# A spectral mixer with a gated feed-forward: the last plain chunk's down stage moves from behind the third new period to behind the second

## The chip, the cores and the metric

The kernel runs on one core of one Trainium2 chip. The metric is the time of one execution on the device in microseconds (us). A core has five engines that run side by side, each with its own queue of instructions: TensorE (PE, matrix products; its weight loads are listed apart as PEld), VectorE (DVE), ScalarE (ACT), GpSimd (POOL) and SyncE (SP, which issues the DMA transfers). [...]

## The reference

The input is x, 8192 tokens of 448 channels, with two blocks that are added to it. The first is spectral: normalise, scale and shift by a condition, transform over the tokens, put each frequency through a small two-layer complex network in 4 blocks of 112 channels, shrink, transform back. The second is a gated feed-forward of 1792 hidden channels. Cut to what matters here:

```python
h = _layernorm(x) * (1 + ca) + sa
x = x + ga * irfft2(mlp(rfft2(h)))              # the spectral block
h = _layernorm(x) * (1 + cb) + sb
x = x + gb * ((gelu(h @ w_gate) * (h @ w_up)) @ w_down)
```

All in float32. The kernel gets that accuracy out of float16 products by writing each operand as a high and a low part: hi·hi + hi·lo + lo·hi, three matmuls for one.

## The kernel before, in words

Up to about 375 us the kernel does the forward transform, the spectral network and the first half of the inverse transform. From there it walks over 32 chunks of 256 tokens (two rows of 128), and this part is what the change touches. For chunk i the work is: the second half of the inverse transform (`inverse` or `winverse`, six matmuls), the residual sum (`residual`), the statistics and the second normalisation (`stats2`, `rsqrt_part` with 13 tiny instructions, `norm2`, all on DVE), packing into high and low float16 parts (`token_sums`, `wpack_hi` on ACT, `wpack_lo` on POOL), transposes by DMA (`wtransposes`), the gate and up products, GELU and product of the two, high and low parts of the result (`quantize`: one ACT instruction for the high part and then one DVE instruction for the low part), and the down stage.

**The down stage** (`down`, L1220) multiplies the 256 tokens' hidden values with `w_down` by a scheme of 7 block products; each product is 7 hidden tiles of three matmuls, 21 matmuls, so a down stage is 147 matmuls. Their results are combined by short ACT, DVE and POOL instructions, and POOL ends with five of them (L1261 and twice L1229, L1230). `down` calls `mid(0)`, `mid(1)` and `mid(2)` between its products: behind the second product, behind the third, and ahead of the last two. There, work of another chunk can be put into the queues.

**Plain and new chunks.** Chunks 0 to 7 are plain: the gate and up products of a chunk go hidden tile by hidden tile (`gate_up`). Chunks 8 to 31 use another block scheme, in *periods*: tile u = 7·i + t has a set of PSUM banks with three regions, and its products come in four stages, `stage_a` (32 matmuls), `stage_b` (10), `stage_c` (24) and `stage_d` (12). One period u (`period`, L1470) interleaves the stages of three tiles: stage a of u, stage d of u−2, stage c of u−1, stage b of u, 78 matmuls. Between a tile's stages other engines read and write its banks: `copy_b` (ACT, L1413) copies two regions out before stage b; `seed` (ACT, L1417) copies one region over another before stage c; `joins` (DVE, L1422 and L1428) reads all three after stage c; only then may stage d add to the first region, because `joins` reads it and stage d overwrites it.

**Order of the work.** From L628 on the instructions of each engine stand in its queue in the order in which the Python code emits them (`tc.manual_schedule()`). A list `held` collects steps that the next period emits behind its `seed`. The loop at L1845 emits, for each u: the period, the pending weight loads (`flush`), the steps of `opening` (chunk 8) or `extra` (later chunks) and, at the third period of a chunk (k = LA = 2), `phase(i)`: the inverse transform, residual and normalisation of chunk i+2 together with the down stage of chunk i−1. In `phase` before, the inverse is ahead of the down stage, and statistics and normalisation are in `mid(0)` to `mid(2)`.

**The seam.** Where the plain chunks end, chunk 7's last two `quantize` calls (tiles 5 and 6) are in `held`, so they are emitted in period 57; period 56 is the first new one, and its function returns early, ahead of `held`. `split_v(10)` and `split_g(10)` make the high and low parts of the operands of chunk 10's inverse (one ACT and one POOL instruction each); they stand in `opening[0]` and `opening[1]`. `phase(8)`, with the down stage of chunk 7, is behind period 58.

**Weights.** The new chunks' weights are in DRAM, 7 tiles of two parts, and in four slots in SBUF. Part 0 of a tile is needed by stages a and b, part 1 by c and d. `after(u, part)` marks a slot's part as free once tile u is done with it, and `flush` issues the next load on SP's queue: tile 60 goes into the slot of 56, 61 into that of 57, 62 into that of 58. The transposes of chunk 9 (five of them, `wtransposes`) are issued on the same queue behind period 58, and chunk 9 begins with period 63.

Of the kernel before, what the change touches and what calls it, by code (L numbers as in the profile page):

```python
# [12 lines left out]
F16 = mybir.dt.float16  # L13
BF16 = mybir.dt.bfloat16
I32 = mybir.dt.int32
AF = mybir.ActivationFunctionType
ALU = mybir.AluOpType
# [7 lines left out]
CB = 2  # L25
# [8 lines left out]
NP = NFT // 2  # L34
# [5 lines left out]
LA = 2  # L40
NSTD = 8
# [8 lines left out]
def spectral_geglu(ctx, tc, x, w1, b1, w2, b2, wg, wu, wd, cvec, wmod, cf1, cs2, cmi, cgm, out):  # L50
    nc = tc.nc
    V, S, G, T = nc.vector, nc.scalar, nc.gpsimd, nc.tensor
# [39 lines left out]
    sa_act = cpool.tile([128, NP], F32, name="sa_act")  # L92
# [235 lines left out]
    with ExitStack() as bctx:  # L328
# [541 lines left out]
        for n, i in enumerate([3, 4, 5, 6, 7, 8, 9, 10, 11, 11, 12, 12, 13, 14]):  # L870
            j, pr = divmod(n, 2)
# [22 lines left out]
        draws, nxt, x1t = {}, {}, {}  # L894
# [3 lines left out]
        def x1_tile(i):  # L898

            x1n[i] = next(n for n in range(len(x1s)) if n not in [x1n.get(j) for j in (i - 1, i - 2, i - 3) if j in x1t])  # L900
            return x1s[x1n[i]]

        cp = None
# [96 lines left out]
    with ExitStack() as cctx:  # L1000
# [54 lines left out]
        def stats2(i, cs=slice(0, D)):  # L1055
            if "st6" not in nxt[i]:
                nxt[i]["st6"] = cp.tile([128, CB, 1, 6], F32, tag="cst6", name="cst6")
                nxt[i]["mv"] = cp.tile([128, CB, 2], F32, tag="cmv", name="cmv")
            st6 = nxt[i]["st6"]
            for b in range(CB):  # L1060
                V.bn_stats(st6[:, b, cs.start // HC], x1t[i][:, b, cs])
            if cs.stop == D:
                for b in range(CB):
                    V.bn_aggr(nxt[i]["mv"][:, b, :], st6[:, b])
# [13 lines left out]
        def rsqrt_part(i, n):  # L1078
            if "r" not in nxt[i]:
                nxt[i]["r"] = rsqrt_steps(cp, nxt[i]["mv"][:, :, 1], CB, "rc")  # L1080
            steps = nxt[i]["r"][1]
            for f in steps[:n]:
                f()
            del steps[:n]

        def norm2(i, b):
            mvt, x1, r = nxt[i]["mv"], x1t[i], nxt[i]["r"][0]
            if b == 0 and i > 0:
                nxt[i]["n"] = ep.tile([128, CB, D], F32, tag="n2", name="n2")
            n = nxt[i]["n"]  # L1090
            V.scalar_tensor_tensor(n[:, b], x1[:, b], mvt[:, b, 0:1], cb_r, op0=ALU.subtract, op1=ALU.mult)
            V.scalar_tensor_tensor(n[:, b], n[:, b], r[:, b : b + 1], sb_r, op0=ALU.mult, op1=ALU.add)
# [96 lines left out]
        def sums(x, e):  # L1189
# [3 lines left out]
            e.tensor_tensor(s3, a11, a21, ALU.subtract)  # L1193
            e.tensor_tensor(s4, a12, s2, ALU.subtract)  # L1194

        def quantize(i, t, cuts=(0, 7)):
            x = acts[(i, t)]
            ac = cp.tile([128, 2, 7, 128], F16, tag="ac", name="ac", bufs=7)
            sc = sa_act[:, t : t + 1]
            for lo, hi in zip(cuts, cuts[1:]):  # L1200
                k = slice(lo, hi)
                S.activation(ac[:, 0, k], x[:, k], AF.Copy, scale=sc)
                V.scalar_tensor_tensor(ac[:, 1, k], x[:, k], sc, ac[:, 0, k], op0=ALU.mult, op1=ALU.subtract)  # L1203
            acts[(i, t)] = ac
# [206 lines left out]
        def copy_b(u):  # L1411
            sbs[u] = cp2.tile([128, 2, 256], F32, tag="sb", name="sb", bufs=2)
            S.copy(sbs[u], sets[u % 3][:, :, 0:256])  # L1413
# [50 lines left out]
        def on(u, f):  # L1464
            if U0 <= u < NT_:
                f(u)
# [3 lines left out]
        def period(u):  # L1470
            on(u, stage_a)
            if u == U0:
                copy_b(u)
                return
            if u == U0 + 1:
                stage_b(U0)
                copy_b(u)
            on(u - 1, seed)
            for fn, *args in held:
                fn(*args)  # L1480
            held.clear()
            on(u - 2, joins)
            on(u - 2, gel3)
            on(u - 4, quant_lo)
            on(u - 2, mult3)
            if u != U0 + 1:
                on(u, copy_b)
            on(u - 2, stage_d)
            on(u - 2, lambda v: after(v, 1))
            on(u - 2, gel1)  # L1490
            on(u - 2, mult1)
            on(u - 2, lambda v: sums(xs[v], G))
            on(u - 3, quant_hi)
            if u == U0 + 1:
                stage_b(u)
                after(U0, 0)
            on(u - 1, stage_c)
            if u != U0 + 1:
                on(u, stage_b)
            on(u, lambda v: after(v, 0))  # L1500

        def winverse(i, ps2):
            nxt[i]["ps"] = [ps2[:, b, 0:D] for b in range(CB)]
            (gh, gl), vh, vl = nxt[i]["g"], nxt[i]["vh"], nxt[i]["vl"]
            for b, ps in enumerate(nxt[i]["ps"]):
                T.matmul(ps, gh[:, b], vh[:, b], start=True, stop=False)
                T.matmul(ps, gl[:, b], vh[:, b], start=False, stop=False)
                T.matmul(ps, gh[:, b], vl[:, b], start=False, stop=True)

        def down_banks(pf):  # L1510
            return lambda q: (pdn[0], pdn[1], pf[:, 0, :], pdn[0], pf[:, 1, :], pdn[1], pdn[0])[q]

        def phase(i):

            u = i * NP + LA
            pf = sets[(u + 1) % 3]
            j = i + 2
            on(u - 3, quant_lo)
            if j < nch:
                winverse(j, pf)  # L1520
                residual(j)
            steps = {
                0: [(stats2,), (rsqrt_part, 5)],
                1: [(rsqrt_part, 9), (norm2, 0)],
                2: [(norm2, 1)],
            }

            def mid(n):
                for fn, *args in steps[n] if j < nch else []:
                    fn(j, *args)  # L1530

            down(i - 1, down_banks(pf), mid)
# [247 lines left out]
        for i in range(NSTD):  # L1780
            if i == 1:
                cctx2.close()
                cctx2 = ExitStack()
                cp2 = cctx2.enter_context(tc.tile_pool(name="cp3", bufs=1))
            for k in range(NFT):
                gate_up(i, k)
                for fn, *args in ahead.pop(i * NFT + k, []):
                    fn(*args)
                if (i, k) == (NSTD - 1, NFT - 1):
                    held += [(quantize, i, t) for t in range(NP - 2, NP)]  # L1790
                elif k % 2 == 1 and i + k > 1:
                    quantize(*((i, k // 2 - 1) if k > 1 else (i - 1, NP - 1)))
                if i == 1:
                    for fn, *args in second.get(k, []):
                        fn(2, *args)
                for fn, *args in prep.pop((i, k), []):
                    fn(*args)
                if k == 2 and i > 0:
                    down(i - 1, two_banks, lambda n: steps_std(i, n))
                if k == 4:  # L1800
                    store_out()
                for fn, *args in first.pop(i * NFT + k, []):
                    fn(*args)
                if (i, k) in ((0, 3), (1, 1)):
                    load_v(i + 2)
                    load_g(i + 2)
                if i == 1 and k == 3:
                    split_g(3)
                    split_v(3)
                if k == 9 and i > 0:  # L1810
                    load_v(i + 3)
                    load_g(i + 3)
                for d, fn, *args in later_by_one(k) if i == 1 else (hooks if i < NSTD - 2 else soon).get(k, []):
                    if i == NSTD - 2 and k < 3 and d == 1:
                        continue
                    if i + d > 2 and i > 0 and (i, k) != (1, 1):
                        fn(i + d, *args)
# [12 lines left out]

        opening = {
            0: [
                (2, split_v),
                (1, norm2, 1),
                (1, token_sums, 0),
                (1, token_sums, 1),
# [2 lines left out]
                (1, wpack_hi, [2]),  # L1839
                (1, wpack_lo, [2]),  # L1840
            ],
            1: [(2, split_g), (1, wpack_hi, [3]), (1, wpack_lo, [3]), (1, wpack_hi, [4]), (1, wpack_lo, [4])],
            2: [(1, wtransposes, range(5))],
        }
        for u in range(U0, NT_ + 1):  # L1845
            period(u)
            i, k = divmod(u, NP)
            if i == nch:
                continue
            if k == LA + 2:  # L1850
                store_out()
            flush()
            for d, fn, *args in opening[k] if i == NSTD and k < 3 else extra[k]:
                if i + d < nch:
                    if fn in (wpack_hi, wpack_lo):
                        held.append((fn, i + d, *args))
                    else:
                        fn(i + d, *args)
            if k == LA:
                phase(i)  # L1860
        store_out()
        late = {
# [80 lines left out]
```

## Time and profile before

| what | value |
|---|---|
| time, median of 3 runs | 1890.91 us (1890.71 to 1893.4) |
| the profiled execution: its own time | 1890.96 us |
| the profiled execution: span from first to last instruction | 1889.2 us |
| granted TensorE clock, mean | 0.996 |
| PE busy | 1848.9 us, 98% of the span |
| PEld busy | 1751.7 us, 93% |
| DVE busy | 1429.5 us, 76% |
| POOL busy | 1266.7 us, 67% |
| ACT busy | 994.4 us, 53% |
| DMA, mean | 175 GB/s |

A row of the timeline gives the start in us from the span's first instruction, the length in us, the engine, the line, the operation, what it writes and reads, its shape and how many of them were merged; in brackets stands how long the engine was idle ahead of it and what ended that. A row of a table of windows gives, for a stretch of time, the busy time and the number of instructions of each engine, then the granted TensorE clock, the DMA share and GB/s. The seam lies at 761.29 us, where the first matmul of L1385 (the new periods) starts.

### The profile page before, as it was taken

Reading aid. Unit: us, or ns where it says so; the run is one execution under the profiler, and the core shown is the slowest. Engines: PE = TensorE matmul, PEld = TensorE weight load, DVE = VectorE, ACT = ScalarE, POOL = GpSimd, SP = SyncE. Lnnn points to the kernel's source line nnn. Section 1 sums busy time; section 2 is a strip of 40 time slices with the busy share of each in tenths; the row PEclk is TensorE's granted clock in tenths of the full one; section 3 lists DMA queues with packets and bytes.
Section 4 is the critical chain, followed back from the end, with each engine's and each line's share of the span. In section 5 each row is a group of like instructions: output and inputs, shape, how many; then the busy total and the mean of one; then the engine's idle time right before and its main releaser. Section 6 shows DMA issues by size and latency. Waiting matters only on the chain.

```text
span 1889.2 us, 56357 instructions
## 1 busy us (share of the span) xinstructions
PE 1848.9 (98%) x23332; PEld 1751.7 (93%) x23332; DVE 1429.5 (76%) x2887; ACT 994.4 (53%) x1844; POOL 1266.7 (67%) x1618
## 2 busy tenths in 40 slices
PE   7899999999999999999999999999999999999998
PEld 3599999878889899999999999999999999999998
DVE  8678788777766667777777777777777777777655
ACT  5677888653444444454554555544554455444443
POOL 3157654347777778777777777777777777777534
PEclk9999999999999999999999999999999999999999
DMA  9999777654544445966666666666666666666651
GB/s 353 316 298 264 205 177 193 185 160 95 133 103 98 99 93 127 296 176 170 169 168 168 168 168 168 168 168 170 177 174 173 169 174 176 176 174 168 162 163 55
DMA packets 380614, 330.49 MB, mean 175 GB/s; under 512 B 110784, under 2 KB 358724, under 8 KB 380356
## 3 DMA queue, kind: packets, MB, share of 16 engines
q1 hardware_dynamic: 380356, 326.87, 63.5%
q8 instruction: 183, 3.00, 0.7%
q14 instruction: 75, 0.61, 0.1%
HBM read 243.32 MB, written 60.10 MB: 161 GB/s over the span
## 4 chain that ended last, share of the span: by engine, by line
PE 77%; DVE 9%; DMA 4%; issue 3%; ACT 3%; POOL 2%; SPq 2%; ACTq 0%; POOLq 0%; DVEq 0%
PE set L1385 34%; PE pgu L1142 10%; PE pdn L1217 6%; PE pdn L1215 6%; PE pdn L1216 6%; PE set L1217 2%; PE set L1216 2%; PE set L1215 2%; DMA xt<-in_A_x 2%; PE ps L211 1%; DVE y L479 1%; DVE x L1438 1%; DVE c L1422 1%; DVE tf L1326 1%; POOL yl L116 1%
## 5 line engine op out<-in xcount | busy, mean ns | idle before, releaser
L1385 PE MATMUL set<-nt,wk 128*128 128x128 f16 x13104 | 742.9, 219 | 3.7 <-DMA wk<-wk 1.6
L1385 PEld LDWEIGHTS <-wk 128*128 128x128 f16 x13104 | 735.6, 98 | 8.9 <-issue 4.8
L1217 PE MATMUL pdn<-wd,ac 128*128 128x224 f16 x1218 | 315.5, 259 | 0.6 <-DVE ac L1203 0.6
L1215 PE MATMUL pdn<-wd,ac 128*128 128x224 f16 x1218 | 315.7, 259 | 0.0
L1216 PE MATMUL pdn<-wd,ac 128*128 128x224 f16 x1218 | 315.5, 259 | 0.0
L1142 PE MATMUL pgu<-nt,wk 128*128 128x256 f16 (+1 forms) x2464 | 269.0, 274 | 3.3 <-DVE x L1183 3.3
L1142 PEld LDWEIGHTS <-wk 128*128 128x128 f16 (+1 forms) x2464 | 226.1, 98 | 44.7 <-issue 18.8
L1434 ACT ACTIVATE gl<-c,dg 128x384 f32<-128x384 f32 x168 | 103.4, 616 | 255.2 <-DVE c L1428 254.2
L1460 DVE SCALAR_TENSOR_TENSOR ac<-x,sa_act,ac 128x896 f16<-128x896 f32 x168 | 212.2, 1263 | 14.7 <-ACT ac L1450 14.7
L1191 POOL TENSOR_TENSOR x<-x 128x128 f32<-128x128 f32 x223 | 130.4, 585 | 120.2 <-DVE x L1183 57.7
L1261 POOL TENSOR_TENSOR cq<-cq 128x224 f32<-128x224 f32 x32 | 21.0, 657 | 262.6 <-DVE cq L1260 262.6
L1438 DVE TENSOR_TENSOR x<-c,gl 128x384 f32<-128x384 f32 x168 | 177.0, 1054 | 17.0 <-ACT gl L1434 17.0
L1450 ACT ACTIVATE ac<-x,sa_act 128x896 f16<-128x896 f32 x168 | 173.5, 1033 | 4.0 <-DVE x L1194 1.3
L1194 POOL TENSOR_TENSOR x<-x 128x128 f32<-128x128 f32 x223 | 170.0, 762 | 0.0
L1215 PEld LDWEIGHTS <-ac 128*128 128x128 f16 x1568 | 153.4, 98 | 4.9 <-issue 4.8
L1217 PEld LDWEIGHTS <-ac 128*128 128x128 f16 x1568 | 153.4, 98 | 0.8 <-DVE ac L1203 0.8
L1216 PEld LDWEIGHTS <-ac 128*128 128x128 f16 x1568 | 153.5, 98 | 0.1
L1193 POOL TENSOR_TENSOR x<-x 128x128 f32<-128x128 f32 x223 | 148.5, 666 | 0.0
L1422 DVE TENSOR_TENSOR c<-set,sb 128x512 f32<-128x512 f32 x168 | 114.9, 684 | 36.1 <-PE set L1385 36.1
L1178 ACT ACTIVATE gel<-pgu,dg 128x256 f32<-128x256 f32 x112 | 49.4, 470 | 158.0 <-PE pgu L1142 150.4
L479 DVE SCALAR_TENSOR_TENSOR y<-pm,t 64x224 f32<-64x224 f32 x256 | 99.5, 389 | 39.1 <-ACT t L471 35.5
L1192 POOL TENSOR_TENSOR x<-x 128x128 f32<-128x128 f32 x223 | 116.9, 524 | 17.5
(336 smaller groups left out, 3987.1 us busy)
## 6 DMA issues: line engine op xcount, KB each, us to landing
wk<-wk SPq DMA_DIRECT2D x76, 1024.0 KB
wk<-wk SPq DMA_DIRECT2D x76, 768.0 KB
vd<-us SPq DMA_DIRECT2D x64, 224.0 KB
xx<-in_A_x SPq DMA_DIRECT2D x32, 448.0 KB
v<-vd SPq DMA_DIRECT2D x63, 224.0 KB
out<-x SPq DMA_DIRECT2D x31, 448.0 KB
xt<-in_A_x SPq DMA_DIRECT2D x15, 896.0 KB
tr<-td SPq DMA_DIRECT2D x60, 224.0 KB
```

The lines of the kernel that those rows point to most:

```text
L1142: T.matmul(pgu[i, t, q][:, pr * H : (pr + 1) * H], ws[rows, n, w, tw], nts[i][rows, tn, :], start=start, stop=stop, skip_group_check=True,)
L1191: e.tensor_tensor(s1, a21, a22, ALU.add)
L1193: e.tensor_tensor(s3, a11, a21, ALU.subtract)
L1194: e.tensor_tensor(s4, a12, s2, ALU.subtract)
L1215: T.matmul(ps, ac[:, 0, ka], w[:, 0, kb], start=n == 0, stop=False)
L1216: T.matmul(ps, ac[:, 0, ka], w[:, 1, kb], start=False, stop=False)
L1217: T.matmul(ps, ac[:, 1, ka], w[:, 0, kb], start=False, stop=n == NP - 1)
L1385: T.matmul(ps2[:, pr, reg * 128 : reg * 128 + 128], slot[:, pr, hl, wt, :], nt[:, xt, :], start=start and j == 0, stop=j == len(terms) - 1 ...
L1422: V.tensor_tensor(c[:, :, 1:3, :], p[:, :, 0:256].rearrange("p g (r c) -> p g r c", r=2), b[:, :, 0:128].rearrange("p g (o c) -> p g o c", ...
L1438: V.tensor_tensor(xs[u][:, 1::3, :], cts.pop(u)[:, 1], gls.pop(u), ALU.mult)
L1450: S.activation(ac[:, 0], xs[u][:, 0:7], AF.Copy, scale=sa_act[:, t : t + 1])
L1460: V.scalar_tensor_tensor(ac[:, 1], xs.pop(u)[:, 0:7], sa_act[:, t : t + 1], ac[:, 0], op0=ALU.mult, op1=ALU.subtract)
```

## The change

Three things move, for chunk 8's first periods alone.

1. Chunk 7's down stage, `phase(8)`, is emitted behind period 57 (k = LA − 1) in place of period 58. Its two borrowed banks are those of the set of tile 58, which has not begun.
2. The `quantize` calls of chunk 7 are spread: tile 5 is quantized in period 56 behind its `copy_b`; the high part of tile 6 (new `quantize_hi`, ACT) goes to `held`, and its low part (new `quantize_lo`, DVE) is emitted at the start of `phase(8)`.
3. In `phase(8)`, `split_g(10)` and `split_v(10)` move from `opening` into `mid(1)`. `winverse(10)` and `residual(10)` move from ahead of the down stage into `mid(2)`. `stats2(10)`, all 13 steps of `rsqrt_part(10)` and both `norm2(10)` move from the three `mid` calls to behind the down stage.

`phase` of all later chunks is as before.

```diff
+        def quantize_hi(i, t):
+            x = acts[(i, t)]
+            ac = cp.tile([128, 2, 7, 128], F16, tag="ac", name="ac", bufs=7)
+            S.activation(ac[:, 0], x[:, 0:7], AF.Copy, scale=sa_act[:, t : t + 1])
+            acts[(i, t)] = ac
+            behind.append((ac, x, t))
+
+        def quantize_lo():
+            for ac, x, t in behind:
+                V.scalar_tensor_tensor(ac[:, 1], x[:, 0:7], sa_act[:, t : t + 1], ac[:, 0], op0=ALU.mult, op1=ALU.subtract)
+            behind.clear()
...
             if u == U0:
                 copy_b(u)
+                quantize(NSTD - 1, NP - 2)
                 return
...
+            if i == NSTD:
+                u = i * NP + LA - 1
+                pf = sets[(u + 1) % 3]
+                quantize_lo()
+                x1t[j] = x1_tile(j)
+                steps = {
+                    0: [],
+                    1: [(split_g,), (split_v,)],
+                    2: [(lambda j: winverse(j, pf),), (residual,)],
+                }
+
+                def mid(n):
+                    for fn, *args in steps[n]:
+                        fn(j, *args)
+
+                down(i - 1, down_banks(pf), mid)
+                stats2(j)
+                rsqrt_part(j, 13)
+                for b in range(CB):
+                    norm2(j, b)
+                return
...
                 if (i, k) == (NSTD - 1, NFT - 1):
-                    held += [(quantize, i, t) for t in range(NP - 2, NP)]
+                    held.append((quantize_hi, i, NP - 1))
...
             0: [
-                (2, split_v),
                 (1, norm2, 1),
...
-            1: [(2, split_g), (1, wpack_hi, [3]), (1, wpack_lo, [3]), (1, wpack_hi, [4]), (1, wpack_lo, [4])],
+            1: [(1, wpack_hi, [3]), (1, wpack_lo, [3]), (1, wpack_hi, [4]), (1, wpack_lo, [4])],
...
-            if k == LA:
+            if k == (LA - 1 if i == NSTD else LA):
                 phase(i)
```

More of the change, by code (lines that the diff above doesn't have):

```diff
@@ L1194, in sums @@
             e.tensor_tensor(s4, a12, s2, ALU.subtract)
+        def quantize_hi(i, t):
[8 more added lines that the diff above has]
+            behind.clear()
+        behind = []
         def quantize(i, t, cuts=(0, 7)):
```

## The prediction

> **What bounds the kernel now.** I read the page first: is there slack on TensorE at all?
>
> ```profile
> span 1889.2 us, 56357 instructions
> PE 1848.9 (98%) x23332; PEld 1751.7 (93%) x23332; DVE 1429.5 (76%) x2887; ACT 994.4 (53%) x1844; POOL 1266.7 (67%) x1618
> ```
>
> PE is busy for 98% of the span, so time is lost where PE waits and nowhere else. The view of waits, for PE from 761 us to the end, has three in all: the two below, and one of the same size in the last chunk, which comes up later.
>
> ```profile
> PE set L1385 <- DMA wk<-wk: 1.6, 1, 1.6
> PE set L1385 <- ACT sb L1413: 0.6, 1, 0.6
> ```
>
> PE's timeline shows both at the seam:
>
> ```profile
> 761.29 4.37 PE L1385 MATMUL set<-nt,wk 128*128 128x128 f16 x74
> 766.22 2.06 PE L1385 MATMUL set<-nt,wk 128*128 128x128 f16 x34 [0.56 <-ACT sb L1413]
> 769.88 4.53 PE L1385 MATMUL set<-nt,wk 128*128 128x128 f16 x78 [1.61 <-DMA wk<-wk]
> 774.22 0.45 PE L1506 MATMUL set<-vh,gh 128*128 128x448 f32 x1
> ...
> 789.62 30.99 PE L1385 MATMUL set<-nt,wk 128*128 128x128 f16 x546
> ```
>
> Period 58 is the row of x78: 4.34 us, 0.0556 us a matmul. The first two rows are stages a of 56 and 57, b of 56 (74 matmuls), then b of 57 and c of 56 (34). From 774.22 to 789.62 runs `phase(8)`: 15.40 us. At the measured rate the 74 end at 765.50 and the 34, from 766.22, at 768.12. So PE loses 0.72 us to `copy_b(57)` and 1.76 us to the weights of tile 58: 2.48 us is all that the seam can give back.
>
> **The gains.** The down stage now runs where PE waited for weights, and stage a of 58 comes some 15 us later: **−1.75**. The other wait begins on ACT:
>
> ```profile
> 763.27 0.58 ACT L1413 COPY sb<-set 128x512 f32<-128x512 f32 x1 [1.31 <-DMA g<-cgm]
> 764.74 0.94 ACT L114 CAST vh<-v 128x896 fp32r<-128x896 f32 x1 [0.89 <-DMA v<-vd]
> 765.59 0.58 ACT L1413 COPY sb<-set 128x512 f32<-128x512 f32 x1
> ...
> 766.37 1.97 ACT L1202 ACTIVATE ac<-x,sa_act 128x896 f16<-128x896 f32 x2
> ```
>
> The cast of `split_v`, itself late for its data, holds `copy_b(57)`. In its place stands the high part of tile 5 (half of L1202's 1.97, 1.0 us), from 763.85 to 764.9. The copy must still wait for stage a of 57, the 64th matmul, at 765.1, and ends at 765.7: **−0.5** of 0.72.
>
> **The moved quantization.** Its low part for tile 6 is the last input of the down stage:
>
> ```profile
> 768.34 2.25 DVE L1203 SCALAR_TENSOR_TENSOR ac<-x,sa_act,ac 128x896 f16<-128x896 f32 x2
> ...
> 784.52 0.69 DVE L1092 SCALAR_TENSOR_TENSOR n<-n,rcy,sb_r 128x448 f32<-128x448 f32 x1
> 785.13 0.38 DVE L1251 TENSOR_TENSOR cq<-pdn,cq 128x224 f32<-128x224 f32 x1
> ...
> 789.83 0.39 DVE L1270 TENSOR_TENSOR cq<-pdn,cq 128x224 f32<-128x224 f32 x1 [1.32 <-PE pdn L1217]
> 790.13 0.68 DVE L1422 TENSOR_TENSOR c<-set,sb 128x512 f32<-128x512 f32 x1
> 790.73 0.41 DVE L1428 TENSOR_TENSOR c<-set,sb 128x256 f32<-128x256 f32 x1
> 791.83 1.42 DVE L1438 TENSOR_TENSOR x<-c,gl 128x384 f32<-128x384 f32 x1 [0.68 <-ACT gl L1434]
> ```
>
> `token_sums`, which ended where L1203 begins (768.34), now ends about 2 us later, as tile 5's low part (half of 2.25, and its wait for ACT) is ahead of it; tile 6's is then ready at 771.5 to 773. PE reaches its use after 36 matmuls of the down stage, which starts at about 767.7: at 0.096 us each, 771.3. Price 0 to 2, and I take **+1.0**, the middle. `split_g` and `split_v` in `mid(1)` cost ACT 0.94 and POOL 2.21 (L116 below) behind the third product, with two short casts before them; the inverse is 42 matmuls (4.0 us) further on and uses that operand last: hidden with little to spare, 0 here, and at most some tenths.
>
> **What is put behind the down stage.** L1251 adds the result of the fourth product. The down stage begins at
>
> ```profile
> 775.53 0.27 PE L1215 MATMUL pdn<-wd,ac 128*128 128x224 f16 x1
> ```
>
> and 84 matmuls on is 783.6; L1251 ran at 785.13, directly behind `norm2` (L1092), which is emitted ahead of it. DVE thus takes its instructions in the order of emission. In the new order that is: L1270 (the last addition of the down stage), then the statistics, 13 steps and `norm2` of chunk 10, then `joins(56)`. And stage d of 56 needs `joins(56)`. That this wait is real is shown by the kernel's last chunk, where PE stops at L1428 and goes on 0.06 us after its end (1866.99 + 0.41 = 1867.40):
>
> ```profile
> 1866.99 0.41 DVE L1428 TENSOR_TENSOR c<-set,sb 128x256 f32<-128x256 f32 x1
> ```
> ```profile
> 1867.46 1.72 PE L1385 MATMUL set<-nt,wk 128*128 128x128 f16 x28 [0.56 <-DVE c L1428]
> ```
>
> Let T be the start of the period behind the down stage (789.62 before). L1422 started at T+0.51, L1428 ended at T+1.52, and stage d is reached after 32 matmuls, at T+1.78: before, 0.2 us of slack. A DVE chain of length L put in between makes PE wait L − 0.2. How long is L? Before, these steps ran with POOL idle:
>
> ```profile
> 780.16:787.50 7.34, 7.34 (x79) 7.34 (x77) 6.54 (x24) 0.62 (x2) 0.00 (x0) 1.00 1.26 298
> ```
>
> 7.34 less the gap with L1251 and L1252 (785.13 to 786.16): L = 6.3. But behind the down stage POOL works without a break: L1229 and L1230 twice, then the `wpack_lo` of `opening[1]` (the three at 772.79), which `held` now brings here, behind the down stage.
>
> ```profile
> 765.82 2.21 POOL L116 TENSOR_TENSOR v<-v,vh 128x896 fp32r<-128x896 f32 x1
> ...
> 772.79 2.50 POOL L1362 TENSOR_TENSOR pk<-tf,pk 128x128 f16<-128x128 f32 x3
> ...
> 791.68 1.15 POOL L1229 TENSOR_TENSOR cq<-cq,gb_r 128x448 f32<-128x448 f32 x1
> 792.91 1.33 POOL L1230 TENSOR_TENSOR x<-cq,x 128x448 f32<-128x448 f32 x1
> ```
>
> DVE's L1438 started at 791.83 and ended at 793.25, 0.42 after this L1229: it had waited for POOL's instruction to end. [...]
>
> From T+2 on, the second L1229, L1230 and the three `wpack_lo` remain: 1.15 + 1.14 + 2.50 = 4.8 us. If every one blocks a DVE step for most of its length, L = 6.3 + 4.3 = 10.6. The ends are 6.3 and 10.6; I take 10.0, near the upper, as the steps are short two-input instructions that meet one POOL instruction after another. So PE waits **+9.8** (6.1 to 10.4).
>
> **The clock.** What follows so long a gap is shown by the table of windows, at the kernel's start and at the seam:
>
> ```profile
> 19.77:22.40 2.63, 0.00 (x0) 0.00 (x0) 2.63 (x15) 1.35 (x3) 0.07 (x1) 1.00 1.01 417
> 22.94:26.35 3.41, 3.35 (x5) 1.71 (x6) 2.90 (x10) 0.88 (x3) 2.91 (x6) 0.50 1.02 420
> 26.35:30.00 3.65, 3.65 (x11) 1.80 (x10) 2.46 (x12) 2.16 (x5) 0.48 (x1) 1.00 1.01 418
> 769.88:774.22 4.34, 4.34 (x78) 4.34 (x79) 2.88 (x5) 2.27 (x5) 4.34 (x7) 1.00 1.10 339
> ```
>
> PE idle for 2.63 us, back at 22.40, and the granted clock was 0.50 from 22.94 to 26.35, then 1.00 again; a gap of 1.61 (the last row) left it at 1.00. After the new gap PE works at half clock until 3.95 us after its return, by this row: half of that is lost, **+2.0**. With part of the slow stretch inside the gap it is less; ends 0.7 and 2.4. [...]
>
> **SP's queue.** The loads (60, part 1) and (62, part 0) wait for stages d and b in period 58, and the transposes stand behind them:
>
> ```profile
> 760.03 20.51 SPq L1301 DMA_DIRECT2D wk<-wk  x8
> 780.59 10.55 SPq L1368 DMA_TRANSPOSE nt<-pk  x5
> ```
>
> With P the end of period 58, the five transposes hold SP until about P+11; then comes (61, part 1), needed by stage c of 61 at P + 3·4.38 + 44·0.056 = P+15.6. That leaves 4.5 us for 0.79 MB: 2.3 us at the 339 GB/s of the last window (no wait), up to 9.85 us as the load issued at 760.03 and awaited until 769.88 (a wait of 5.3, but with more loads in flight). I take **+0.5**, near the lower end. The transposes themselves are due at period 63, P+17.5.
>
> **The sum**: −1.75 − 0.5 + 1.0 + 9.8 + 2.0 + 0.5 = +11.05 us on the profiled execution's 1890.96 (span 1889.2 and 1.8 around it; the runs' median, 1890.91, is the same): **1902.0 us**, 0.6% slower. Nothing behind the seam gives it back: in the 1100 us that follow PE has one wait of 0.6 us.
>
> **The rivals.**
> 1. *The chain runs at its price with POOL idle, and most of the half clock lies inside the gap*: −2.25 + 1.0 + 6.1 + 0.7 = +5.55, **1896.5 us**. For it: POOL may as well be the one that waits. Against: the row of L1438.
> 2. *The clock stays up*: 2.0 less, **1900.0**. Against: the row of 2.63 us.
> 3. *SP's queue binds*: the load takes as long as the one at 760.03, 4.8 more than in the sum, **1906.8**. For it: the transposes fill SP. Against: less traffic by then.
> 4. *Not slower*: `joins(56)` does not wait, as DVE gets through most of chunk 10's steps ahead of L1270, in the 1.3 us in which it is idle and before. Then −2.25 + 1.0 = −1.25, **1889.7**. It decides if at least 4.9 of the 6.3 us of steps run ahead of L1270 (what is left, less 0.2, must stay under the net gain of 1.25). Against: L1251 at 785.13.
>
> **How the numbers follow.** Forecast 0.57, rival 1 0.17, rival 2 0.07, rival 3 0.08, rival 4 0.11. The range holds the forecast with its ends (−2.5 + 0 + 6.1 + 0.7 + 0 = +4.3, 1895.3; −2.25 + 2 + 10.4 + 2.4 + 2 = +14.6, 1905.5) and rivals 1 and 2, and leaves out rivals 3 and 4: 1895.0 to 1905.5. Under 0.2%, 3.8 us, a difference can't be told from none: rival 4 is almost all "same"; a gain of 0.2% would need more than the 2.48 us there are. Faster 0.02, same 0.09, slower 0.89.
>
> **What would show it.** PE's wait for `L1428` with 8 to 10 us at about 785 us, and none for weights before it; `stats2` behind L1270; two-input DVE steps of 0.16 us stretched up to POOL's; a granted clock of 0.50 around 795; a short wait for `ac` at 771. The prediction is wrong if L1422 starts right behind L1270, or if PE's wait is there and the time is not.

## The result and the profile after

The changed kernel takes 1902.1 us (median, 1900.35 to 1902.55), the kernel before on the same chip 1891.38 us (1890.71 to 1893.4): a ratio of 1.0055, with a 95% interval of 1.0043 to 1.0066. The change makes the kernel 0.55% slower; the prediction was 1902.0 us. The profiled execution of the changed kernel took 1900.35 us, its span is 1898.6 us, its mean granted clock 0.995.

A row of the page and, below it, the view of waits for PE from 755 us to the end:

```profile
PE 1851.0 (97%) x23332; PEld 1754.1 (92%) x23332; DVE 1429.9 (75%) x2887; ACT 995.5 (52%) x1844; POOL 1262.7 (67%) x1618
```
```profile
PE set L1399 <- DVE c L1442: 9.8, 2, 9.2
PE set L1521 <- DVE cq L1266: 0.6, 1, 0.6
```

The two waits of before, for the weights and for the copy, are gone. In their place stands one of 9.2 us for `joins(56)` (the other 0.6 of the first row is the one in the last chunk, as before), and one of 0.6 us at the inverse (L1521), which the prediction did not have. The lines have moved: new periods L1385 → L1399, `joins` L1422, L1428 → L1436, L1442, the down stage's last addition L1270 → L1284. (In the runs below that edit more they move again: the new periods are L1402 and `joins` L1439, L1445 in pool_away, L1401 and L1438, L1444 in the three `early` runs.)

PE's timeline of the changed kernel, and one row of the kernel before, the first matmul of the next inverse, as the end of the stretch to compare:

```profile
760.75 6.54 PE L1399 MATMUL set<-nt,wk 128*128 128x128 f16 x108
767.13 0.26 PE L1229 MATMUL pdn<-wd,ac 128*128 128x224 f16 x1
...
777.98 0.45 PE L1521 MATMUL set<-vh,gh 128*128 128x448 f32 x1 [0.63 <-DVE cq L1266]
...
783.33 1.95 PE L1399 MATMUL set<-nt,wk 128*128 128x128 f16 x32
794.48 35.69 PE L1399 MATMUL set<-nt,wk 128*128 128x128 f16 x592 [9.20 <-DVE c L1442]
829.97 0.45 PE L1521 MATMUL set<-vh,gh 128*128 128x448 f32 x1
```
```profile
820.42 0.45 PE L1506 MATMUL set<-vh,gh 128*128 128x448 f32 x1
```

From the first matmul of the new periods to this inverse, the same matmuls take 820.42 − 761.29 = 59.13 us before and 829.97 − 760.75 = 69.22 us after. This stretch is called the seam below; it is 10.09 us longer, and each part can be read from the rows:

| part of the seam | before, us | after, us | difference |
|---|---|---|---|
| stages a, b of 56 and 57, c of 56 (108 matmuls) | 761.29 to 768.12 | 760.75 to 767.13 | −0.45 |
| wait for the weights of tile 58 | 768.12 to 769.88 | none | −1.76 |
| down stage with the inverse | 774.22 to 789.62 | 767.13 to 783.33 | +0.80 |
| wait for `joins(56)`, from 783.33 + 32·0.0556 = 785.11 | none | 785.11 to 794.48 | +9.37 |
| the other 624 matmuls | 4.34 + 30.80 | 1.78 + 35.49 | +2.13 |
| sum | 59.13 | 69.22 | +10.09 |

The two executions differ by 9.39 us in their own times: the one of after came to the seam 0.54 us earlier, and 0.16 us lie elsewhere. Where the seam starts differs by some us between executions of kernels that are alike up to there (759.88 us in the run norm_later, 763.31 in pool_away), so the experiments are read by the seam first and by their times second.

Why `joins(56)` is late is seen on DVE and POOL at the same time:

```profile
768.88 1.57 DVE L1205 SCALAR_TENSOR_TENSOR ac<-x,sa_act,ac 128x896 f16<-128x896 f32 x1
...
777.45 0.39 DVE L1266 TENSOR_TENSOR cq<-set,cq 128x224 f32<-128x224 f32 x1 [1.68 <-PE set L1231]
...
783.53 0.39 DVE L1284 TENSOR_TENSOR cq<-pdn,cq 128x224 f32<-128x224 f32 x1 [1.32 <-PE pdn L1231]
783.84 1.14 DVE L1061 BATCH_NORM_STATS2 cst<-x 128x6 f32<-128x448 f32 x2
...
785.51 1.05 DVE L126 TENSOR_SCALAR rcy<-rcve 128x2 int32<-128x2 int32 x1
...
786.67 1.10 DVE L128 TENSOR_SCALAR rcve<-rcve 128x2 f32<-128x2 f32 x1
...
788.81 1.08 DVE L132 TENSOR_TENSOR rct<-rcy 128x2 f32<-128x2 f32 x1
...
793.41 0.68 DVE L1436 TENSOR_TENSOR c<-set,sb 128x512 f32<-128x512 f32 x1
794.01 0.41 DVE L1442 TENSOR_TENSOR c<-set,sb 128x256 f32<-128x256 f32 x1
```
```profile
785.41 1.13 POOL L1243 TENSOR_TENSOR cq<-cq,gb_r 128x448 f32<-128x448 f32 x1
786.62 1.13 POOL L1244 TENSOR_TENSOR x<-cq,x 128x448 f32<-128x448 f32 x1
787.71 2.16 POOL L1376 TENSOR_TENSOR pk<-tf,pk 128x128 f16<-128x128 f32 x3
```

Behind the down stage's last addition (L1284) come the statistics, the 13 steps and `norm2` of chunk 10, and only then `joins` (L1436): 793.41 − 783.84 = 9.57 us. PE goes on 0.06 us after L1442's end. Three of the little steps of 128x2 elements take 1.05 to 1.10 us, and each of these ends within 0.03 us of the end of a POOL instruction: L126 at 786.56 and L1243 at 786.54, L128 at 787.77 and L1244 at 787.75, L132 at 789.89 and the last L1376 at 789.87.

The table of windows shows the clock: full for 4.18 us of the gap, then half, until 5.2 us after PE's return.

```profile
785.28:789.46 4.18, 0.00 (x0) 0.00 (x0) 4.01 (x8) 0.00 (x0) 4.10 (x6) 1.00 0.00 0
789.46:799.70 10.24, 5.22 (x50) 5.22 (x50) 6.59 (x16) 1.52 (x4) 2.15 (x5) 0.50 0.20 59
799.70:805.00 5.30, 5.30 (x98) 5.30 (x97) 2.92 (x7) 3.58 (x9) 2.26 (x6) 1.00 0.83 242
```

In the 5.22 us there were 50 matmuls where 94 fit at 0.0556 us: 2.4 us. The seam shows 2.13, 0.3 less; before, 546 matmuls took 30.80 us where 30.36 are due at that rate, and where the difference comes from was not shown.

### The profile page after: what moved, and what is told of

It is laid out like the page before. It is cut to its first block, busy times and chain, and to the rows that moved or that the text cites. A ratio compares the mean times of both kernels' runs of the same rounds, so it can differ in the third digit from the quotient of the medians.

```text
span 1898.6 us, 56358 instructions
## 1 busy us (share of the span) xinstructions
PE 1851.0 (97%) x23332; PEld 1754.1 (92%) x23332; DVE 1429.9 (75%) x2887; ACT 995.5 (52%) x1844; POOL 1262.7 (67%) x1618
## 4 chain that ended last, share of the span: by engine, by line
PE 79%; DVE 9%; DMA 3%; ACT 3%; issue 3%; POOL 1%; SPq 1%; ACTq 0%; DVEq 0%; POOLq 0%
PE set L1399 36%; PE pgu L1142 11%; PE pdn L1231 6%; PE pdn L1229 6%; PE pdn L1230 6%; PE ps L211 2%; PE set L1231 2%; PE set L1229 2%; PE set L1230 2%; DVE y L479 1%; DVE x L1452 1%; DVE c L1436 1%; DMA raw<-in_B_w_up 1%; DVE wk L838 1%; DMA raw<-in_B_w_gate 1%
## 5 line engine op out<-in xcount | busy, mean ns | idle before, releaser
L1399 PE MATMUL set<-nt,wk 128*128 128x128 f16 x13104 | 744.9, 219 | 10.8 <-DVE c L1442 9.8
L1399 PEld LDWEIGHTS <-wk 128*128 128x128 f16 x13104 | 738.0, 98 | 15.6 <-issue 13.7
L1436 DVE TENSOR_TENSOR c<-set,sb 128x512 f32<-128x512 f32 x168 | 115.0, 684 | 38.6 <-PE set L1399 38.6
```

The source lines that it names most:

```text
L1399: T.matmul(ps2[:, pr, reg * 128 : reg * 128 + 128], slot[:, pr, hl, wt, :], nt[:, xt, :], start=start and j == 0, stop=j == len(terms) - 1 ...
L1436: V.tensor_tensor(c[:, :, 1:3, :], p[:, :, 0:256].rearrange("p g (r c) -> p g r c", r=2), b[:, :, 0:128].rearrange("p g (o c) -> p g o c", ...
```

## The experiments

The kernel before ran beside each of them on the same chip: 1891.04 us beside the first four, 1890.96 us beside the last four. "Seam" is the stretch above, read from one profiled execution of each run; before has 59.13 us, the changed kernel 69.22 us. The intervals of joins_first, pool_away, fill and norm_later overlap that of the changed kernel, 1.0043 to 1.0066, so what these four change is told by the seam and the rows, and not proved by the times.

| run | what is edited | time, us | ratio to before | seam, us |
|---|---|---|---|---|
| joins_first | changed: `joins(56)` ahead of the chain | 1898.63 | 1.0040 [1.0026, 1.0054] | 66.87 |
| pool_away | changed: POOL's work moved away from the chain | 1898.90 | 1.0039 [1.0023, 1.0054] | 66.29 |
| fill | changed: PE kept busy in the gap | 1901.16 | 1.0053 [1.0040, 1.0067] | 67.76 |
| norm_later | changed: `norm2` out of the chain | 1897.61 | 1.0038 [1.0025, 1.0052] | 67.15 |
| chain_late | before: the chain behind the down stage, nothing else | 1900.97 | 1.0052 [1.0038, 1.0065] | 69.37 |
| early | changed: the chain back inside the down stage | 1893.65 | 1.0014 [1.0005, 1.0023] | 60.72 |
| early_order | early, transposes behind one more load | 1889.50 | 0.9994 [0.9985, 1.0003] | 58.31 |
| early_tr | early, transposes in the down stage | 1889.51 | 0.9991 [0.9982, 1.0000] | 57.61 |

**Is it the chain alone?** chain_late is the kernel before with one thing of the change.

```diff
-                for fn, *args in steps[n] if j < nch else []:
+                for fn, *args in steps[n] if j < nch and i > NSTD else []:
                     fn(j, *args)
...
+            if i == NSTD:
+                stats2(j)
+                rsqrt_part(j, 14)
+                norm2(j, 0)
+                norm2(j, 1)
```

> The kernel before, with chunk 10's stats2, its thirteen small steps and norm2 put behind the down stage of the last plain chunk and nothing else moved: the down stage stays behind the third new period, the inverse behind its end. Theory (what costs is that this chain stands behind the down stage, wherever that stands): the two waits of before stay (0.56 us for the copy, 1.61 us for the weights), TensorE waits about 8 us for the joins (chain about 8.3 us, with the four POOL instructions of the finish in its way), the half clock costs about 2.1 us, the seam from stage a's first product of the second new chunk to the inverse of the last takes about 69.4 us, a profiled execution about 1901 us. Rival (the chain is only harmful together with the earlier down stage): no wait for the joins, seam 59.1 us, 1891 us.

The seam meant there is the stretch defined above. The view of waits, and one row each of PE's and DVE's timeline:

```profile
PE set L1385 <- DVE c L1428: 8.3, 2, 7.7
PE set L1385 <- DMA wk<-wk: 1.6, 1, 1.6
PE set L1385 <- ACT sb L1413: 0.4, 1, 0.4
```
```profile
799.89 31.65 PE L1385 MATMUL set<-nt,wk 128*128 128x128 f16 x514 [7.72 <-DVE c L1428]
```
```profile
790.74 1.14 DVE L1061 BATCH_NORM_STATS2 cst<-x 128x6 f32<-128x448 f32 x2
...
798.82 0.68 DVE L1422 TENSOR_TENSOR c<-set,sb 128x512 f32<-128x512 f32 x1
```

The theory holds: both waits of before stand, the chain takes 798.82 − 790.74 = 8.08 us, PE waits 7.7 us for it, and the seam is 10.24 us longer than before. So it is not the earlier down stage that costs; one chunk's normalisation ahead of another chunk's `joins` on DVE costs as much as the whole change.

**Is it the order on DVE?** joins_first takes the changed kernel and emits `joins(56)` ahead of the chain.

```diff
-            on(u - 2, joins)
+            if u != U0 + 2:
+                on(u - 2, joins)
...
                 down(i - 1, down_banks(pf), mid)
+                on(U0, joins)
                 stats2(j)
```

> joins(56) is emitted ahead of chunk 10's statistics, 13 steps and norm2, all else as in the changed kernel. Theory (the queue position on DVE behind that chain is what holds stage d): PE's wait of 9.2 us for joins(56) goes, and stage d of tile 57 waits instead, as joins(57) still stands behind the chain: about 6.9 us (1.0 + 9.6 of chain + 0.9 + 1.0 behind T+0.5, against stage d of 57 at T+6.2). The profiled time falls by some 2.5 us, from 1900.4 to about 1897.9. Rival (PE waits there for something else, a bank or a copy): the wait of 9.2 us stays where it is and so does the time.

```profile
784.39 4.52 PE L1399 MATMUL set<-nt,wk 128*128 128x128 f16 x78
795.50 33.38 PE L1399 MATMUL set<-nt,wk 128*128 128x128 f16 x546 [6.60 <-DVE x L1459]
```
```profile
795.16 0.28 DVE L1459 TENSOR_TENSOR x<-set,gl 128x128 f32<-128x128 f32 x1
```

PE's first wait is gone: period 58 passes whole (78 matmuls in 4.52 us). But at its end, 46 matmuls past the place of the first stop, PE stops for 6.6 us. It waits for L1459, the last step that reads tile 56's banks, which stage a of tile 59 overwrites; L1459 now stands behind the chain and ends at 795.44. The expectation had named stage d of 57 and `joins(57)`, which would have come 32 matmuls later: the kind of wait was right, the step was not. The seam gets 2.35 us shorter. PE goes on 33.67 us after the seam's start, and 33.73 us in the changed kernel: the end of the chain decides when, and what is put ahead of it decides how much PE has done by then.

**How much of the chain is POOL?** pool_away leaves DVE's order alone. It moves the four `finish` instructions and the three `wpack_lo` on POOL (with the `wpack_hi` on ACT that belong to them; in the changed kernel these end at 776.08, well ahead of the chain).

```diff
+                if i == NSTD - 1:
+                    tail.append((finish, b, h, G))
+                    continue
...
+            if u == U0 + 2:
+                for fn, *args in tail:
+                    fn(*args)
...
-                    if fn in (wpack_hi, wpack_lo):
+                    if fn in (wpack_hi, wpack_lo) and u != U0 + 1:
```

> POOL's work is taken out of the stretch in which the chain runs: the wpack_lo of opening[1] is emitted ahead of the down stage, and the last four POOL instructions of chunk 7's down stage behind period 58. Theory (POOL's instructions block DVE's steps): the chain takes 6.3 us in place of 9.6, PE's wait falls from 9.2 to about 6.0, and the profiled time to about 1897.1. Rival (the chain is long of itself): chain, wait and time stay.

DVE and POOL in this run:

```profile
786.40 1.14 DVE L1061 BATCH_NORM_STATS2 cst<-x 128x6 f32<-128x448 f32 x2
...
787.99 0.17 DVE L126 TENSOR_SCALAR rcy<-rcve 128x2 int32<-128x2 int32 x1
...
788.27 0.16 DVE L128 TENSOR_SCALAR rcve<-rcve 128x2 f32<-128x2 f32 x1
...
792.67 0.68 DVE L1439 TENSOR_TENSOR c<-set,sb 128x512 f32<-128x512 f32 x1
```
```profile
784.94 0.65 POOL L1275 TENSOR_TENSOR cq<-cq 128x224 f32<-128x224 f32 x1
795.00 0.45 POOL L1191 TENSOR_TENSOR x<-x 128x128 f32<-128x128 f32 x1 [9.41 <-DVE x L1455]
```

With POOL idle from 785.59 to 795.00 the same chain takes 792.67 − 786.40 = 6.27 us in place of 9.57, and the steps of 1.05 and 1.10 us take 0.17 and 0.16. So 3.3 us of the wait are POOL's instructions, and 6.3 the steps themselves. PE's wait is 5.9 us, the seam 2.93 us shorter. The profiled time, 1900.04 us, did not fall to the 1897.1 expected, as this execution came to the seam 2.56 us later than that of the changed kernel.

**Is it the chain's length?** norm_later takes the four `norm2` instructions out of it.

```diff
                 rsqrt_part(j, 13)
-                for b in range(CB):
-                    norm2(j, b)
...
+            if u == U0 + 2:
+                for b in range(CB):
+                    norm2(i + 2, b)
```

> The changed kernel with norm2 of chunk 10 alone taken out of the chain, to behind the third new period. Theory: the chain ahead of the joins is shorter by norm2's four steps, 2.7 us: TensorE's wait for the joins falls from 9.2 to about 6.5 us, the seam from 69.2 to about 66.5 us, the profiled time to about 1897.6 us. Rival (the joins are held by something else than the length of the chain): wait and seam unchanged, 1900 us.

```profile
PE set L1399 <- DVE c L1442: 7.1, 2, 6.6
PE set L1399 <- DMA wk<-wk: 0.7, 1, 0.7
```

The wait falls by 2.6 us, as expected. The seam falls only by 2.07: PE comes 0.7 us too early for a load of weights, which the longer wait had hidden.

**What does the clock cost?** fill gives PE 150 products in the gap; nobody reads their result, and nothing of the computation is left out.

```diff
+        def fill(u, n):
+            for _ in range(n):
+                T.matmul(pdn[0][:, 256:384], wslot[slot_of[u]][:, 0, 0, 0, :], nts[u // NP][:, 0, :], start=True, stop=True, skip_group_check=True)
...
+            if u == U0 + 2:
+                fill(u, 150)
```

> 150 matmuls of 128 columns, whose result nobody reads, are put between stage a of tile 58 and stage d of tile 56, so that PE works through 8.3 us of the 9.2 us for which it waited. Theory (half a clock behind the gap costs some 2.1 us of its own): the granted clock stays at 1.00, the seam up to chunk 11's inverse takes 67.1 us in place of 69.2, and the profiled time is about 1898.3. Rival (the lower clock costs nothing, as PE is not the bound there): 69.2 us and 1900.4.

PE's timeline, and a row of windows right behind the gap:

```profile
787.28 8.54 PE L1486 MATMUL pdn<-nt,wk 128*128 128x128 f16 x150
796.68 18.25 PE L1399 MATMUL set<-nt,wk 128*128 128x128 f16 x324 [0.86 <-DVE c L1442]
815.74 15.14 PE L1399 MATMUL set<-nt,wk 128*128 128x128 f16 x268 [0.81 <-DMA wk<-wk]
```
```profile
796.68:800.00 3.32, 3.31 (x60) 3.31 (x60) 1.87 (x4) 1.75 (x5) 1.74 (x4) 1.00 0.22 65
```

The clock stays at 1.00 (from 787.28 to 800.00 us) and the seam is 1.46 us shorter, not the 2.1 expected: again a wait of 0.8 us for weights comes up. Without it the seam would be 66.95, 2.27 us shorter than in the changed kernel. The ratios to before, 1.0053 and 1.0055, can't tell the two kernels apart; the seams do.

**Can the earlier down stage be had without the chain?** early leaves the down stage behind the second period and puts the chain back into its `mid` calls; for that the inverse must come earlier, behind the first product.

```diff
+                    if not last and m == 0:
+                        mid(-1)
...
-                    0: [],
-                    1: [(split_g,), (split_v,)],
-                    2: [(lambda j: winverse(j, pf),), (residual,)],
+                    -1: [(lambda j: winverse(j, pf),), (residual,)],
+                    0: [(stats2,), (rsqrt_part, 5)],
+                    1: [(rsqrt_part, 9), (norm2, 0)],
+                    2: [(norm2, 1)],
...
-                stats2(j)
-                rsqrt_part(j, 13)
-                for b in range(CB):
-                    norm2(j, b)
...
-                    held.append((quantize_hi, i, NP - 1))
+                    held += [(split_v, i + 3), (split_g, i + 3), (quantize_hi, i, NP - 1)]
```

> The down stage stays behind period 57, but the inverse of chunk 10 is ahead of most of it (behind the first of its products, with split_v and split_g in held behind seed) and statistics, steps and norm2 are in mid(0) to mid(2) again. Theory (moving the down stage costs nothing, only the chain behind it does): no wait for joins(56), none for the weights of tile 58, clock 1.00; the seam takes 57 to 58 us against 59.1 before, and the profiled time is 1888.8 to 1889.8, a gain of about 0.1% over the kernel before. Rival (the early down stage is itself at fault, by SP's queue or by what it pushes back): 1890.9 or more, with a new wait.

Expected was a seam of 57 to 58 us; it is 60.72, and the kernel is 0.14% slower than before. PE's and SP's timeline say why:

```profile
770.32 0.47 PE L1524 MATMUL set<-vh,gl 128*128 128x448 f32 x1 [1.03 <-POOL gl L116]
...
806.57 15.14 PE L1401 MATMUL set<-nt,wk 128*128 128x128 f16 x268 [2.37 <-DMA wk<-wk]
```
```profile
788.92 11.98 SPq L1384 DMA_TRANSPOSE nt<-pk  x5
801.00 0.54 SPq L1317 DMA_DIRECT2D wk<-wk  x1
```

The wait for `joins` is gone (0.2 us left), but the load (61, part 1) stands behind the five transposes, goes out at 801.00, and PE, which needs it, gets it at 806.57. That is the wait of the prediction's third rival, in a kernel in which PE is no longer some 10 us late. A smaller wait, of 1.03 us, is for the low part of the gates (POOL, L116) at the inverse, which now comes early; the theory of the expectation had neither, its rival had named SP's queue. Two runs test it: early_order issues the transposes behind that load, early_tr issues them inside the down stage, when SP has nothing else.

```diff
             # early_order
-            2: [(1, wtransposes, range(5))],
+            2: [],
...
+            if u == U0 + 3:
+                wtransposes(i + 1, range(5))
```

> The kernel of the run before (down stage behind the first new period) with the five transposes of chunk 9's pieces issued later on SP's queue, behind the load that they held up; the order on the compute engines stays. Theory (the load (61, part 1) came late because it stood behind the transposes on SP): TensorE's wait of 2.4 us for a DMA goes (0 to 1 us may be left for the next load), seam about 58.3 us instead of 60.7, profiled time 1889.5 to 1890. Rival (the load is late for another reason, its buffer for instance): the wait stays, seam 60.7 us.

The period meant there is 57, the second of the new ones, as in `early`.

```diff
             # early_tr
-                    0: [(stats2,), (rsqrt_part, 5)],
+                    0: [
+                        (stats2,),
+                        (rsqrt_part, 5),
+                        (lambda j: wpack_hi(j - 1, [3, 4]),),
+                        (lambda j: wpack_lo(j - 1, [3, 4]),),
+                        (lambda j: wtransposes(j - 1, range(5)),),
+                    ],
...
-            1: [(1, wpack_hi, [3]), (1, wpack_lo, [3]), (1, wpack_hi, [4]), (1, wpack_lo, [4])],
-            2: [(1, wtransposes, range(5))],
+            1: [],
+            2: [],
...
-                    held += [(split_v, i + 3), (split_g, i + 3), (quantize_hi, i, NP - 1)]
+                    held += [(split_g, i + 3), (split_v, i + 3), (quantize_hi, i, NP - 1)]
```

> The same kernel with the transposes issued earlier instead: chunk 9's pieces are packed and transposed in the middle of the stage, while SP has nothing to issue, and the split of the gates stands ahead of the split of the values. Theory: no wait for a DMA, a wait of 0.4 to 1.0 us for the gates, seam about 58.2 us against 59.1 before, profiled time 1889.5 to 1890, a gain too small to be told from before by the times alone. Rivals: the wait of 2.4 us stays (60.7 us), or a new wait of TensorE for VectorE takes its place, because the packing now stands among VectorE's other work in the down stage (60 us or more).

PE in early_order, then PE and SP in early_tr:

```profile
799.60 20.27 PE L1401 MATMUL set<-nt,wk 128*128 128x128 f16 x358 [0.19 <-DVE c L1444]
```
```profile
768.60 0.47 PE L1525 MATMUL set<-v,gh 128*128 128x448 f32 x1 [0.82 <-POOL v L116]
...
781.89 35.00 PE L1401 MATMUL set<-nt,wk 128*128 128x128 f16 x624
```
```profile
774.02 10.74 SPq L1384 DMA_TRANSPOSE nt<-pk  x5
```

In both the wait for the load is gone; early_order, which changes nothing but the order on SP's queue, shows that this order was its cause. In early_order the wait of 1.03 us for the gates stays; early_tr splits the gates first and has one of 0.82 us for the values (L1525), where the expectation had one for the gates. The seams are 58.31 and 57.61 us, and in early_tr the 624 matmuls behind the down stage pass without a stop. That is 1.5 us less than before in the seam, and 1889.51 against 1890.96 us in the medians: both agree, but the interval of the ratio, 0.9982 to 1.0000, touches 1, so the gain over the kernel before is not proved by the times. Against the changed kernel the seam is 11.6 us shorter.

## Why the prediction was right, and where it was not

The mechanism is the one named: chain_late, pool_away and norm_later show it from three sides. That the forecast of 1902.0 us met 1902.1 to 0.1 us is luck. The sum of +11.05 us stands against +10.09 in the seam, 9.39 between the two profiled executions and 10.72 between the medians (1902.1 and 1891.38), and it came that close because errors of both signs met.

- *The gains, −1.75 and −0.5*: measured −1.76 and −0.45. Right. (In the prediction's reading of the rows of before, 74 matmuls at 0.0556 us from 761.29 end at 765.40, not 765.50, so the wait for `copy_b(57)` was 0.82 us and the two together 2.58; of the first, some 0.4 us were left.)
- *The low part of tile 6, +1.0*: measured 0. L1205 was done at 770.45; PE came to its use after 36 matmuls, 767.13 + 3.46 = 770.6, and has no wait there. `token_sums` was expected to end 2 us later than before and ended 0.5 us later (768.96 against 768.42). The prediction overlooked what it took away itself: before, one of its steps lay beside POOL's part of `split_v` (L116, 765.82 to 768.03) and took 2.14 us, and with `split_v` moved the same step (now L1345) took 0.47.

```profile
766.11 2.14 DVE L1331 TENSOR_TENSOR tf<-n,tf 128x192 f32<-128x192 f32 x1
```

- *The split and the inverse in `mid`, 0*: missed by +0.8. The prediction weighed when the inverse's operand is ready, and not its bank. L1521 starts at 777.98, 0.14 us after the end of L1266, which reads a bank that the inverse writes, and about 1 us after its last operand (L116 on POOL, done at 777.01); ahead of the down stage the inverse had no such reader. A step that moves has to be asked for its output too.
- *PE's wait for `joins(56)`, +9.8*: measured 9.37. The step that was a little off is L: 9.57 us for the 10.0 taken. Its lower end, 6.3, is what pool_away measured (6.27). Of the 10.0, 3.7 were POOL's; it is 3.3, as the first steps (L1061, 1.14 us for two) were not held up and had POOL's first instructions beside them.
- *The clock, +2.0*: measured +2.13 in the seam, about 2.3 by fill. The size was right, the time behind it was not: half rate lasted 5.2 us past PE's return and not 3.95. That it came out alike is luck: half of 5.22 would be 2.6, and the matmuls lost were fewer. The prediction does not say from what its ends of 0.7 and 2.4 come.
- *SP's queue, +0.5*: 0 in the changed kernel. There the load went out only at 808.84, as SP's row shows, and yet nobody waited, as PE itself was some 10 us late; it came to this load at about 815.1 (268 matmuls ahead of 829.97), 6.2 us after the issue, so with little to spare:

```profile
800.14 8.60 SPq L1382 DMA_TRANSPOSE nt<-pk  x5
808.84 0.55 SPq L1315 DMA_DIRECT2D wk<-wk  x1
```

The price is real as soon as PE is less late: 0.7 us in norm_later, 0.8 in fill, 2.4 in early. The load took 5.6 to 6.8 us from its issue to the matmul that needed it, so the bound of 2.3 us from the bandwidth of a busy window, near which the prediction put itself, was the wrong one.

Rival 1 (chain at its price with POOL idle) is what pool_away builds, and the trace of the changed kernel excludes it. Rival 2 (clock stays up) is excluded by the row of 0.50. Rival 3 (SP's queue binds, 1906.8) did not come about in this kernel, as PE has no wait for a load in it. Rival 4 (`joins` does not wait) is excluded by L1436 starting behind the whole chain. Of what was to be seen, all was there but the short wait for `ac` at 771 us, and the wait for L1428 of before, now L1442, came with 9.2 us.

## What to carry to other kernels

What is emitted ahead of the step that another engine needs next can become that engine's wait (here 9.57 us of chain ahead of `joins(56)` on DVE made PE wait 9.20 us): before moving a block, list for every engine what comes to stand ahead of the next step that TensorE waits for, and price that, not the moved block. Where a moved stage drags a dependent chain to the stage's end, split it and leave the chain under the stage, even if its head has to go earlier (here the seam is 11.6 us shorter in early_tr than in the changed kernel). And when one wait goes, look at once for the next: here a load behind transposes cost nothing under a stall of 9 us, and 2.4 us without it.

## What the runs showed of the hardware beyond the expectation

- DVE steps with one input of 128x2 elements (L126, L128: 0.17 and 0.16 us in pool_away) were held for 1.05 and 1.10 us beside POOL's L1243 and L1244 of 1.13 us; the prediction had expected that of steps with two inputs only. L1061, a statistics step with one input, kept its 1.14 us for two (783.84 to 784.98) beside L1243 and L1244 (783.11 to 785.45), the same as in pool_away with POOL idle. Why the one was held and the other not was not shown.
- The clock fell to half 4.18 us after PE's last matmul in the changed kernel, but 2.13 us after it in joins_first (788.91 to 791.04) and 5.09 in pool_away (787.84 to 792.93). What is alike is the length of the stretch at half rate, 10.24 us in the changed kernel and joins_first, 6.82 in norm_later and pool_away: three times and twice the 3.41 us of the stretch that starts at 22.94 us in the kernel before. In the changed kernel an earlier stretch at half rate starts at 379.86 us, 409.60 us (40 times 10.24) ahead of the one at 789.46. What sets these lengths and the moment of a change was not shown. In joins_first, norm_later and pool_away:

```profile
791.04:801.28 10.24, 5.78 (x55) 5.78 (x55) 6.08 (x17) 2.03 (x4) 3.07 (x7) 0.50 0.87 189
```
```profile
788.68:795.50 6.82, 4.52 (x43) 4.52 (x43) 5.15 (x14) 1.45 (x3) 2.91 (x5) 0.50 0.22 53
```
```profile
792.93:799.75 6.82, 6.02 (x57) 6.01 (x57) 2.62 (x6) 2.31 (x5) 4.59 (x7) 0.50 0.36 115
```

  At 0.0556 us a matmul 104, 81 and 108 would have fit behind PE's return where 55, 43 and 57 were done, a loss of 2.7, 2.1 and 2.8 us, against 2.4 in the changed kernel: with waits of 6.6, 6.6, 5.9 and 9.2 us, a shorter gap saved the wait and not the clock.
- Five transposes of chunk 9's pieces held SP's queue for 8.6 us in the changed kernel, 12.0 in early and 10.7 in early_tr; in the last two the row of the first starts before POOL had packed the pieces (done at 790.55 and 775.74), so some 1.6 and 1.7 us of this are a wait for POOL. The load behind them went out 0.1 us after they were through: 808.74 and 808.84 us in the changed kernel, where PE did not wait for it, 800.90 and 801.00 in early, where PE waited 2.4 us.
